# Two copies of the first group's kT, from VectorE to ScalarE

## The chip, the cores and the metric

The kernel runs on one core of one Trainium2 chip. A core has a matrix engine (TensorE, PE in the profile, with its weight loads as PEld), VectorE (DVE), ScalarE (ACT), GpSimd (POOL) and a queue engine (SyncE, SP), and 16 DMA engines. The metric is the device time of one launch in microseconds, as the median of several runs; a profile of one execution shows what each engine did.

## The reference

Sliding-window attention with four sink positions, then an MLP mixer over tokens and channels. Cut to what matters (B = 4 batches, H = 8 heads, S = 768 positions, D = 64):

```python
def _attn_ref(q, k, v, n_sink, window):        # n_sink = 4, window = 128
    scores = scale * np.matmul(q, k.transpose(0, 1, 3, 2))
    rel = pos[:, None] - pos[None, :]
    keep = (pos[None, :] < n_sink) | ((rel >= 0) & (rel < window))
    scores = np.where(keep, scores, -1000000000.0)
    a = np.exp(scores - max)
    a = a / (np.sum(a, axis=-1, keepdims=True) + 1e-09)
    return np.matmul(a, v)

def _moe_ref(x, w_tok1, w_tok2, w_ch1, w_ch2):  # x: heads side by side, 4 x 768 x 512
    xt = x.transpose(0, 2, 1)
    h = np.maximum(xt @ w_tok1, 0.0) @ w_tok2   # 768 -> 256 -> 768
    u = x + h.transpose(0, 2, 1)
    h2 = np.maximum(u @ w_ch1, 0.0) @ w_ch2     # 512 -> 1536 -> 512
    return u + h2
```

## The kernel before

The work is cut into eight groups of four heads (two groups make a batch), and a group into two pairs of heads (j = 0, 1). For each pair q and k are loaded as float32, cast to bfloat16, transposed by TensorE into a PSUM bank, and copied from there into qT and kT. Then come the scores, 128 keys at a time with the 256 queries that can see them, in three units a pair; an exp from PSUM into pT; and the product with v.

Which engine does the PSUM copies of the first batch stands in a table: one row for each pair (2 * group + j), and in it the engine of q and that of k. A tuple leaves the choice to a scheduler.

```python
FIRST_TURNS = [[('ACT', 'DVE'), 'ACT'], [('ACT', 'DVE'), 'DVE'], ['DVE', 'DVE'], ['DVE', 'ACT']]
SPLIT_TC = {(0, 1), (0, 0)}              # pairs whose copies are made in two halves
SIZES = [1, 1, 2, 2, 2, 2, 2, 3]         # units of scores in one task, by group
PE_MASKS = {(0, 1), (1, 0), (1, 1), (0, 0)}
...
# make_turn: six transposes into one bank, then the copies
m = add("PE", pe(*[P] * m_), f, [c[x] if parts > 1 else c, t_ident], prio=pr(g, "tr", j), need=("g", 1), slot=slot)
...
if (g, j) in SPLIT_TC:
    ...
    for y in range(2):
        G.T[w][j].append(add(FIRST_TURNS[2 * g + j][w], either(NT * P // 2), lambda t, y=y, eh=eh: eh(t, y), [m, *free],
                             prio=pr(g, "tc", j) + 0.01 * y, slot=slot, frees=y == 1))
    continue
```

In the first batch the mask is put in by TensorE: a product of the identity with a tile of large negative numbers (`mneg`) opens the accumulation, and the four score products go on top. The last task of a group also makes the scores of the sink positions from `ks`, two small copies out of kT, which wait for all of the group's kT:

```python
def f(t, todo=todo, slots=slots, first=first, early=early, fm=fm, sink_slot=sink_slot):
    if first and not early:
        fm(t)                                            # ident x mneg, two matmuls
    for (j, u), slot in zip(todo, slots):
        for kt, w in kts_of(u)[0]:
            for i in range(2):
                nc.tensor.matmul(half(slot, i)[:, at:at + w]..., qkT(kT, g, j)[...], qkT(qT, g, j)[...], ...)
    if sink_slot:
        for c in range(4):
            nc.tensor.matmul(flat(sink_slot)..., ks[s][...], qkT(qT, g, c % 2)[...], start=True, stop=True)
...
G.exp[j, u] = add("ACT", act(2 * w), e, [m, *oldpv], prio=pr(g, "ex", j), slot=slot, frees=True)
```

Scores go through two double banks (`ps_sa`, `ps_sb`), everything else through four single banks (`ps_ga` to `ps_gd`). A score unit can begin when the exp of the unit before it in its buffer is done. The product with v needs the exps, v, and for the later rows the sink values (`pka`, `vsink`):

```python
m = add("PE", cost, f, [*deps, *G.cv, *(G.burst if last else [])], prio=pr(g, "pv"), need=("x" if last else "g", 1), slot=slot)
```

v and the weights are loaded through GpSimd's queue, each such load waiting for the one eight places before it:

```python
LOADS = "v0 v1 tok1 ch1a ch1c tok2 ch1b ch2b k2 ch2a q2 v2 q3 k3 v3".split()
...
if eng == "POOL" and len(log) >= 8:
    deps.append(log[-8])
```

The order of instructions on each engine isn't written by hand. All work is added as tasks with dependencies, a priority (a long table of ranks) and an estimated length, and a greedy scheduler plays them through and writes down the order. The engines then run that fixed order, waiting where an input isn't there:

```python
t.prio = r                       # from the table of ranks
...
todo = plan.order()              # plays the tasks through by estimated lengths
for t in todo:
    t.fn(t)
```

So a change of an engine in one entry can move other instructions too, where the scheduler comes to another order.

Of the kernel before, what the change touches and what calls it, by code (L numbers as in the profile page):

```python
# [15 lines left out]
LOADS = "v0 v1 tok1 ch1a ch1c tok2 ch1b ch2b k2 ch2a q2 v2 q3 k3 v3".split()  # L16
CAST_LOADS = set()
HALVES = set()
FIRST_TURNS = [[('ACT', 'DVE'), 'ACT'], [('ACT', 'DVE'), 'DVE'], ['DVE', 'DVE'], ['DVE', 'ACT']]
K_QUEUE = ['ACT', 'ACT', 'ACT', 'ACT']  # L20
PE_MASKS = {(0, 1), (1, 0), (1, 1), (0, 0)}
DMA_TURNS = {5, 6, 7}
# [120 lines left out]
class Plan:  # L143
# [8 lines left out]
    def add(self, *a, **k):  # L152
        t = Task(*a, **k)
        self.tasks.append(t)
        return t
# [182 lines left out]
def either(n):  # L338
    return {"ACT": act(n) + ACT_MORE, "DVE": dve(n)}
# [3 lines left out]
def kernel(  # L343
# [282 lines left out]
    def pr(g, what, j=0):  # L626
        like = KIND.get(what, what)
        extra = BIAS.get(f"{what}{g}", 0) + (BIAS.get(f"{what}{g}.{j}", 0) if j else 0)
        if what == "ex" and g >= GB:
            extra += 20  # L630
        if g < GB:
            return FIRST[like] + 0.5 * g + extra
        return (g // GB) * 10 + CH[like] + 0.5 * (g % GB) + extra
# [91 lines left out]
    def make_turn(g, w):  # L725
# [11 lines left out]
        for j in range(2):  # L737
# [3 lines left out]
            for x in range(parts):  # L741
# [20 lines left out]
                if (g, j) in SPLIT_TC:  # L762
                    def eh(t, y, j=j, slot=slot):
                        ps = flat(slot).bitcast(BF16)[:, 0:NT * P].rearrange("d (t p) -> d p t", t=NT)
                        hp = P // 2
                        copy(t, T[s][:, ts(j, NT)].rearrange("d t p -> d (t p)").rearrange("d (p t) -> d p t", t=NT)[:, ds(hp * y, hp)], ps[:, ds(hp * y, hp)])
# [6 lines that stand above are left out]
                G.T[w][j].append(add(FIRST_TURNS[2 * g + j][w] if g < GB else ("ACT", "DVE"), either(m_ * P), e, [m, *free], prio=pr(g, "tc", j), slot=slot, frees=True))  # L773

# [745 lines left out]
```

## Time and profile before

| | us |
|---|---|
| time, median of 3 runs | 200.34 (200.27 to 200.4) |
| span of the profiled execution | 198.6 |
| VectorE busy | 137.8 |
| ScalarE busy | 109.0 |
| GpSimd busy | 84.8 |
| v of group 0, issue to landing | 13.5 |
| VectorE's two copies that the change concerns, 10.28 to 11.29 | 1.01 |

The profile names an instruction by its line in the kernel, its engine and what it writes and reads: L753 are the transposes, L443 copies and casts on VectorE or GpSimd, L441 those on ScalarE, L815 and L819 the masks, L832 the scores, L876 the exps, L863 the exp of the sink scores, L839 the sink scores, L936, L941 and L945 the products with v, L1011 and L1035 the token mixing, L1113 the channel mixing. Letters at the end of a name tell copies of a tile apart: kTa belongs to the even groups, kTb to the odd ones, pTa and pTb to the two pairs of an even group, pTc and pTd to those of an odd one. Start times are in us from the start of the span. A bracket at the end of a row says how long the engine stood idle before it and what ended that.

### The profile page before, as it was taken

What the parts mean: (1) busy time and instruction counts of PE and PEld (TensorE: products, weight loads), DVE (VectorE), ACT (ScalarE), POOL (GpSimd) and SP (SyncE); (2) the same over time, 40 slices, a digit from 0 to 9 for tenths busy, and PEclk for the clock granted to TensorE, in tenths of its full rate; (3) what the DMA queues carried; (4) which work ended last, traced back from release to release, by engine and by line L of the source; (5) the groups of instructions that cost most, each with busy time, mean ns of one, the idle gap of its engine ahead of it and who ended that gap; (6) DMA issues with size and microseconds to landing.
All of it is one profiled execution on the core that took longest, in us unless ns stands there. A gap on an engine that the chain in (4) does not pass through costs nothing.

```text
span 198.6 us, 4636 instructions
## 1 busy us (share of the span) xinstructions
PE 190.0 (96%) x1784; PEld 129.3 (65%) x1795; DVE 137.8 (69%) x323; ACT 109.0 (55%) x196; POOL 84.8 (43%) x148
## 2 busy tenths in 40 slices
PE   7788999999999999999999999999999999999992
PEld 2433786665667564665766787566778787567882
DVE  4598673567775668834568965468588969289973
ACT  2787558889999744187436201867846002855100
POOL 8995432005899953178571010892970000020000
PEclk9999999999999999999999999999999999999999
DMA  5999999999399979899999899250000149000043
GB/s 172 367 224 181 208 207 329 234 257 218 91 317 214 206 150 140 215 129 225 231 179 133 158 206 208 106 137 0 0 3 0 38 99 314 30 3 0 26 162 132
DMA packets 75015, 31.00 MB, mean 156 GB/s; under 512 B 63666, under 2 KB 71474, under 8 KB 74994
## 3 DMA queue, kind: packets, MB, share of 16 engines
q1 hardware_dynamic: 44082, 18.85, 42.0%
q0 software_dynamic: 29680, 10.22, 42.0%
q10 hardware_dynamic: 1232, 1.64, 2.3%
q8 instruction: 14, 0.23, 0.5%
q14 instruction: 7, 0.06, 0.1%
HBM read 26.77 MB, written 6.29 MB: 167 GB/s over the span
## 4 chain that ended last, share of the span: by engine, by line
PE 88%; DMA 7%; ACT 2%; issue 1%; DVE 1%; POOL 0%; DVEq 0%; POOLq 0%
PE ps_gb L1113 9%; PE ps_gd L1113 7%; PE ps_ga L1113 7%; DMA vaa<-in_v_dram 7%; PE ps_gd L1260 5%; PE ps_gb L1260 5%; PE ps_gc L1113 4%; PE ps_gc L1260 4%; PE ps_ga L1260 3%; PE ps_sa L1260 3%; PE ps_gd L1368 3%; PE ps_gc L1368 3%; PE ps_sa L832 2%; PE ps_sb L832 2%; PE ps_sb L1113 2%; PE ps_gd L1011 2%
## 5 line engine op out<-in xcount | busy, mean ns | idle before, releaser
L1113 PEld LDWEIGHTS <-w_ch 128*128 128x128 bf16 x352 | 33.1, 98 | 20.3 <-issue 0.6
L1260 PEld LDWEIGHTS <-v 128*128 128x128 bf16 x222 | 21.1, 98 | 4.1 <-issue 0.5
L1070 ACT ACTIVATE v<-ps_gb 128x384 bf16<-128x384 f32 x18 | 8.9, 493 | 12.8 <-PE ps_gb L1113 12.7
L1070 ACT ACTIVATE v<-ps_gc 128x384 bf16<-128x384 f32 x12 | 5.9, 491 | 16.0 <-PE ps_gc L1113 15.1
L1197 POOL TENSOR_SCALAR v<-q32b 128x384 bf16<-128x384 f32 x1 | 1.2, 1176 | 27.6 <-DVE q32b L1183 27.6
L887 POOL TENSOR_TENSOR pTa<-pTa,mask 128x512 bf16<-128x512 bf16 x2 | 2.3, 1155 | 21.9 <-ACT pTa L876 21.9
L1113 PE MATMUL ps_gd<-uTa,w_ch 128*128 128x384 bf16 x56 | 11.4, 326 | 0.0
L1070 ACT ACTIVATE v<-ps_ga 128x384 bf16<-128x384 f32 x18 | 8.8, 491 | 4.7 <-PE ps_ga L1113 4.6
L1113 PE MATMUL ps_gb<-uTa,w_ch 128*128 128x384 bf16 x56 | 11.4, 326 | 0.0
L1011 PEld LDWEIGHTS <-w_tok 128*128 128x128 bf16 x96 | 9.2, 98 | 1.8
L1070 ACT ACTIVATE v<-ps_gd 128x384 bf16<-128x384 f32 x15 | 7.4, 492 | 5.3 <-PE ps_gd L1113 5.0
L1368 PEld LDWEIGHTS <-v 128*128 128x128 bf16 x72 | 6.2, 98 | 6.2 <-issue 0.8
L1113 PE MATMUL ps_gb<-uTb,w_ch 128*128 128x384 bf16 x48 | 9.8, 326 | 0.0
L1072 DVE TENSOR_SCALAR v<-ps_gd 128x384 bf16<-128x384 f32 x7 | 3.9, 555 | 7.6 <-PE ps_gd L1113 7.6
L486 POOL DMA_DIRECT2D vaa<-in_v_dram x4 | 6.0, 1504 | 7.4 <-PE ps_gc L945 7.4
L1113 PE MATMUL ps_ga<-uTa,w_ch 128*128 128x384 bf16 x44 | 8.9, 326 | 0.0
L486 POOL DMA_DIRECT2D vab<-in_v_dram x4 | 5.8, 1453 | 6.2 <-PE ps_gb L1035 2.3
L1113 PE MATMUL ps_ga<-uTb,w_ch 128*128 128x384 bf16 x40 | 8.1, 326 | 0.0
L876 ACT ACTIVATE pTc<-ps_sb 128x768 bf16<-128x768 f32 (+1 forms) x6 | 5.5, 921 | 3.5 <-PE ps_sb L832 3.5
L876 ACT ACTIVATE pTb<-ps_sa 128x1024 bf16<-128x1024 f32 (+1 forms) x7 | 6.9, 989 | 0.5 <-PE ps_sa L832 0.5
L443 POOL CAST kbb<-k32b 128x768 bf16<-128x768 f32 x5 | 4.4, 884 | 5.5 <-DMA k32b<-in_k_dram 5.5
L443 POOL CAST qbb<-q32b 128x768 bf16<-128x768 f32 x5 | 4.4, 888 | 5.3 <-DMA q32b<-in_q_dram 5.3
(460 smaller groups left out, 587.9 us busy)
## 6 DMA issues: line engine op xcount, KB each, us to landing
q32a<-in_q_dram SPq DMA_DIRECT2D x4, 384.0 KB, 4.4
vaa<-in_v_dram POOLq DMA_DIRECT2D x4, 384.0 KB, 11.4
vab<-in_v_dram POOLq DMA_DIRECT2D x4, 384.0 KB, 11.4
w_ch<-in_moe_w_ch_dram POOLq DMA_DIRECT2D x3, 512.0 KB, 15.3
w_ch<-in_moe_w_ch_dram POOLq DMA_DIRECT2D x2, 768.0 KB, 19.7
q32b<-in_q_dram SPq DMA_DIRECT2D x8, 192.0 KB, 4.0
k32b<-in_k_dram SPq DMA_DIRECT2D x8, 192.0 KB, 3.7
out_dram<-oa SPq DMA_DIRECT2D x4, 256.0 KB, 3.5
```

The source lines that it names most:

```text
L443: on(t).tensor_copy(out=o, in_=i)
L486: t = add(eng, hold, lambda t: e.dma_start(out=o, in_=i), deps, prio=prio, dma=work, run=run)
L832: nc.tensor.matmul(half(slot, i)[:, at:at + w].rearrange("p (c q) -> p c q", q=P), qkT(kT, g, j)[ds(64 * i, 64), kt], qkT(qT, g, j)[ds(64 ...
L876: nc.scalar.activation(dst[:, :, 512 * u:512 * u + w], ps_s[slot.at[1]][:, :, 0:w], AF.Exp, scale=scale)
L887: on(t).tensor_tensor(out=dst[:, :, 0:2 * P], in0=dst[:, :, 0:2 * P], in1=mask0.rearrange("p i c q -> p i (c q)"), op=ALU.mult)
L1011: nc.tensor.matmul(flat(slot)[:, 0:GH * D], w_tok1[:, n, ts(tt, P)], x[:, n, ds(a * GH * D, GH * D)], start=(n == 0), stop=(n == NT - 1))
L1070: nc.scalar.activation(o, i, AF.Relu)
L1072: nc.vector.tensor_scalar(out=o, in0=i, scalar1=0.0, scalar2=None, op0=ALU.max)
L1113: nc.tensor.matmul(flat(slot)[:, 0:HS], w_ch1[:, c, ts(ft, P)], uT_[:, c, ds(half * HS, HS)], start=(c == 0), stop=(c == NC - 1))
L1197: nc.gpsimd.tensor_scalar(out=o, in0=i_, scalar1=0.0, scalar2=None, op0=ALU.max)
L1260: nc.tensor.matmul(flat(slot)[:, 0:cw], A[n][0][:, x, ts(i, P)], W[n][:, x, ds(c0, cw)], start=(first and x == 0), stop=(x == NH - 1), ski ...
L1368: nc.tensor.matmul(flat(slot)[:, 0:cw], v1[:, ft, ts(st, P)], w_ch2[:, ft, ds(c0, cw)], start=(ft == 0), stop=(ft == NF - 1 and (b > 0 or ...
```

## The change

One entry of the table: the copy of kT of group 0, second pair of heads, goes from VectorE to ScalarE. The pair is one of those that are copied in halves, so two instructions of 128x384 elements change engines. It is meant to take load from VectorE in the first microseconds, where it casts, copies and moves constants for both groups of the first batch. (The change carries the name "normalising of the last batch's attention in two tasks, ranks refitted"; that code and the ranks are the same in both kernels, and what differs is only this line.)

```diff
-FIRST_TURNS = [[('ACT', 'DVE'), 'ACT'], [('ACT', 'DVE'), 'DVE'], ['DVE', 'DVE'], ['DVE', 'ACT']]
+FIRST_TURNS = [[('ACT', 'DVE'), 'ACT'], [('ACT', 'DVE'), 'ACT'], ['DVE', 'DVE'], ['DVE', 'ACT']]
```

The scheduler makes a somewhat different order of it, in the first 20 us alone. Written as tasks, in order:

```
TensorE, before                          TensorE, after
scores group 0, pair 1, unit 0           scores group 0, pair 1, unit 0
scores group 0, pair 1, unit 1           transposes q, group 1, pair 0
transposes q, group 1, pair 0            scores group 0, pair 1, unit 1
transposes k, group 1, pair 0            transposes k, group 1, pair 0
scores group 0, pair 1, unit 2, sinks    scores group 0, pair 1, unit 2, sinks
transposes q, group 1, pair 1            transposes q, group 1, pair 1
product with v, group 0 (8 matmuls)      scores group 1, pair 0, 384 wide
transposes k, group 1, pair 1            product with v, group 0 (8 matmuls)
scores group 1, pair 0, 384 wide         transposes k, group 1, pair 1
scores group 1, pair 0, 512 wide         scores group 1, pair 0, 512 wide
```

On ScalarE the exp of the 384-wide unit of group 1 likewise goes ahead of the kT copy of group 1's second pair, and one of its two small copies into `ks` of group 0 goes to VectorE; one small copy for group 1 goes one place later. On VectorE, beside the copies taken away, the first normalising products stand one place apart among the constants' copies. GpSimd and SyncE keep their order.

## The prediction

> **What bounds the kernel now.** I read the page first, then the waits of TensorE, then the first 31 us in order of time, then GpSimd's queue of loads. The page says who is full:
>
> ```profile
> span 198.6 us, 4636 instructions
> ...
> PE 190.0 (96%) x1784; PEld 129.3 (65%) x1795; DVE 137.8 (69%) x323; ACT 109.0 (55%) x196; POOL 84.8 (43%) x148
> ...
> PE 88%; DMA 7%; ACT 2%; issue 1%; DVE 1%; POOL 0%; DVEq 0%; POOLq 0%
> ```
>
> TensorE has 8.6 us without a matmul, and the chain that ends last is 88% TensorE and 7% one transfer. Of the 8.6 us, 3.6 lie behind the last matmul (stores), 2.2 before the first 6 us are over. An entry that moves two copies from one half-empty engine to another can only matter in the few gaps left. TensorE's waits name them:
>
> ```profile
> PE ps_ga L1475 <- DVE warm L447: 1.2, 1, 1.2
> PE ps_ga L753 <- DVE kba L443: 1.1, 1, 1.1
> PE ps_gb L941 <- DMA vaa<-in_v_dram: 0.9, 1, 0.9
> PE ps_sa L819 <- ACT pTc L876: 0.4, 1, 0.4
> ```
>
> Columns: total, times, longest. The first two come before the changed copies. The third is the one to look at: TensorE stands 0.9 us because the first product of probabilities and v, which is next in its fixed order, needs v of group 0. That load is issued at 1.55 and takes 13.5 us (the DMA's 7% of the chain). The surroundings, in order of time (start, length, engine):
>
> ```profile
> 10.28 1.01 DVE L443 COPY kTa<-ps_gd 128x384 bf16<-128x384 bf16 x2
> 11.46 1.00 ACT L876 ACTIVATE pTb<-ps_sa 128x1024 bf16<-128x1024 f32 x1
> 13.74 0.51 PE L753 MATMUL ps_gd<-ident,qbb 128*128 128x128 bf16 x6
> 13.86 0.38 ACT L863 ACTIVATE pka<-ps_gc 128x256 bf16<-128x256 f32 x1 [0.49 <-PE ps_gc L839]
> 15.15 0.20 PE L941 MATMUL ps_gb<-vaa,pTa 128*128 128x65 bf16 x1 [0.90 <-DMA vaa<-in_v_dram]
> 15.40 0.50 PE L753 MATMUL ps_gc<-ident,kbb 128*128 128x128 bf16 x6
> 15.74 0.49 PE L819 MATMUL ps_sb<-mneg,ident 128*128 128x384 bf16 x2
> 15.94 0.81 ACT L441 ACTIVATE kTb<-ps_gc 128x768 bf16<-128x768 bf16 x1 [0.99 <-PE ps_gc L753]
> 16.43 0.39 PE L819 MATMUL ps_sa<-mneg,ident 128*128 128x512 bf16 x1
> 16.65 0.81 ACT L876 ACTIVATE pTc<-ps_sb 128x768 bf16<-128x768 f32 x1
> 17.70 1.02 ACT L876 ACTIVATE pTc<-ps_sa 128x1024 bf16<-128x1024 f32 x1
> 20.54 0.28 PE L936 MATMUL ps_gd<-vsink,pka 128*128 128x260 bf16 x1
> ```
>
> The first row is the two copies that the change moves. The gap ahead of 15.15 holds back TensorE, and ScalarE with it (0.99 us idle before 15.94). From 15.94 to 20.5 the two go hand in hand, exp after exp through two score buffers; from 20.54 on TensorE is full (7.60 of 7.60 us between 24.0 and 31.6).
>
> **What the Trainium skill says.** *Perfetto Trace Analysis*, Optimizing Scalar/DVE Operations: every instruction pays an access overhead, about 51 ns for ScalarE on PSUM and 125 ns for VectorE on PSUM, the recorded latency is longer because its tail overlaps the next instruction, and work may be moved to ScalarE where VectorE is full. The trace agrees for ScalarE: a 384-wide copy is recorded with 0.49 us, but the next instruction starts 0.37 us after it (8.04 to 8.41). On VectorE the two copies, from 10.28, let the next one start at 11.21, 0.465 each, less than 384 elements at its 0.96 GHz plus 125 ns (an estimate from that page and *VectorE: DVE Perf Modes*, Specifications: 0.525). The measured values are used. *VectorE: DVE Perf Modes*, the perf-mode tier table, allows copies from PSUM up to double rate; 0.465 us for 384 elements is 1.2 ns an element, so no doubling shows here, and VectorE is no faster than ScalarE at this copy. *Perfetto Trace Analysis*, Optimization Strategy: look for gaps on the fullest engine and make the dependency start sooner. The change can't make v land sooner; it can only put other work into the gap.
>
> **The change part by part.** Comparing the compiled orders, all that differs lies in the first 20 us; from there on each engine has the same instructions in the same order (bank names apart). GpSimd and SyncE don't change at all.
>
> 1. VectorE loses two 384-wide copies, 0.93 us (10.28 to 11.21), and gains one 64x8 copy for the sink keys, about 0.15. It casts group 1's q and k from about 10.3 rather than 11.21. It then stands until ScalarE's second half copy is done (step 2: 11.8), so its copies of group 1's first q and k start near 12.0 and 12.95, against 12.74 and 13.61: some 0.65 earlier.
>
> 2. ScalarE gains two copies of 0.37 and loses one of the small copies, (11.46 - 11.13)/2 = 0.165: net +0.58 us. Start to start, with 0.91 for a 1024-wide exp (8.41 to 9.32), 0.97 for the one before 10.29, 0.70 for a 768-wide one (an estimate from its 0.81 less 0.11 overlap), 0.28 for the sink exp (13.86 to 14.14): half copy 10.29, exp 10.66, half copy 11.36 (ending 11.85), exp of the next unit 11.73 (before 11.46), small copy, exp 12.80 (before 12.36), sink exp 13.9, exp 14.18 (before 14.14). Two idle stretches, 0.49 and 0.99 us in the rows above, take up the 0.58.
>
> 3. TensorE's order changes in two places. The second score unit of group 0's second pair of heads goes behind one batch of six transposes, which covers the later kT. And the 384-wide score unit of group 1 (the rows at 15.74) goes ahead of the product that waits for v. It needs kT of group 1 (step 1, about 13.9), and its buffer, free when the exp from 12.80 ends at 13.82. The six transposes at 13.74 precede it, so masks near 14.12, scores near 14.54 (16.16 - 15.74 = 0.42 later, as now), done by 14.9. That is before v lands at 15.10.
>
> 4. So after v lands TensorE still does the product (15.15) and six transposes (15.40), but at 15.74 it goes straight to the unit that now starts at 16.43: **0.69 us** of its work moves into the gap. ScalarE's 0.81 us exp of that unit (now 16.65) likewise moves into its gap, near 15.0. The kT copy stays at 15.94; the next exp starts near 16.8 instead of 17.70.
>
> 5. From there the alternation runs on. The exps now at 18.63, 19.74 and 20.66 come near 17.85, 18.8 and 19.9 (0.91 an exp, 0.17 for the small copy; 0.85 to 0.95 for a unit of TensorE), and TensorE is through with that unit near 19.8 instead of 20.54. VectorE's sink values, now ready at 18.37 + 1.29 = 19.66, are a floor just under that. Lead at this place: **0.74 us**.
>
> 6. From 20.54 on TensorE is its own limit, so the lead lives to the end unless a load, which doesn't move, becomes the last to arrive. The sum: 200.34 - 0.74 = 199.60; I take off 0.05 for the tight places of the third rival: **199.65 us**.
>
> **The rivals.** *First: ScalarE becomes the bound.* It is full between 8 and 12 (3.96 of 4.00 us), and gets 0.58 more there; were there no idle time after it, every exp would come 0.3 to 0.6 later, and with them the units behind: 200.6 to 200.9. Against it: the 0.49 and 0.99 us of idle time just behind, and step 2, where the delay is down to 0.04 by 14.18.
>
> *Second: VectorE's relief is worth nothing.* If kT of group 1 or the exp that frees the score buffer is late, the unit isn't done when v lands; then TensorE finishes it first, and the product comes later by as much as was saved. A unit started only at 15.0 would give 200.3. For it speaks that the margin in step 3 is only 0.2 us; against it, that each bit done before 15.10 is still won.
>
> *Third: the loads hide it.* GpSimd's queue keeps at most eight loads open, so its issues show when earlier ones land:
>
> ```profile
> 27.16 0.75 POOL L486 DMA_DIRECT2D k32b<-in_k_dram  x1 [1.12 <-DMA w_tok<-in_moe_w_tok_dram]
> 30.23 1.43 POOL L486 DMA_DIRECT2D vab<-in_v_dram  x1 [2.32 <-PE ps_gb L1035]
> ```
>
> The first waits for the second token weight: issued at 10.45, it takes 16.4 us, so it lands at 26.85. TensorE's first use is at 27.66, and would be at 26.9: nothing to spare. The issue at 30.23 waits, by the eight-load rule, for the third part of the channel weight; TensorE's first use, at 31.4, would move to 30.65. k of group 2 lands at 35.4 and is cast by 36.4; its transposes, at 37.3, would move to 36.5. All three just fit a lead of 0.74; a lead of 1 us would be cut. If one lands later than now, the time comes back to 199.8 to 200.2.
>
> **Range and chances.** The gap is 0.9 us, which caps the direct gain: 199.4, or 199.2 if ScalarE's idle time is used better than I think. Rival two or three in part gives 199.9 to 200.2. Eight in ten: 199.2 to 200.25. Two per cent are 4.0 us; nothing in the first 20 us that the change touches has that size, so within 2% has 0.98, and 0.01 on either side.
>
> **What would show it.** Right: group 1's 384-wide scores ahead of 15.1, TensorE's wait for v near 0.2 us (from 0.9), ScalarE's exp of them near 15.0, the sink product that starts at 20.54 now near 19.8, and a wait-free TensorE after it. Wrong: these scores behind 15.1 (step 3), exps behind 16 us no earlier than now (steps 2, 5), or a new wait of TensorE for a weight near 27, 31 or 36.5 (step 6). A longer v load would also break it, as everything hangs on its landing at 15.1.

## The result, and the profile after

The changed kernel takes 199.35 us (199.29 to 199.49) beside 200.37 us (200.27 to 200.5) for the kernel before, a ratio of 0.995 with a 95% interval of 0.9932 to 0.9967: about 1.0 us less. The page of the changed kernel:

```profile
span 197.8 us, 4635 instructions
...
PE 190.4 (96%) x1784; PEld 129.4 (65%) x1795; DVE 136.4 (69%) x322; ACT 109.3 (55%) x197; POOL 84.9 (43%) x148
```

Nothing of weight is different in the sums. VectorE is 1.4 us less busy and ScalarE 0.3 us more, TensorE has 7.4 us without a matmul instead of 8.6. The span is 0.8 us shorter, not 1.0: the profiled execution of the kernel before was its fastest (200.27), that of the changed one its slowest (199.49). TensorE's wait for v is still there, 0.6 us instead of 0.9, and its 0.4 us wait for an exp (`ps_sa L819 <- ACT pTc` in the prediction's list) is gone. The stretch in order of time (start, length, engine):

```profile
10.21 0.52 ACT L441 ACTIVATE kTa<-ps_gd 128x384 bf16<-128x384 bf16 x1
...
11.28 0.55 ACT L441 ACTIVATE kTa<-ps_gd 128x384 bf16<-128x384 bf16 x1
...
11.89 0.96 DVE L443 COPY qTb<-ps_gb 128x768 bf16<-128x768 bf16 x1
...
13.00 0.96 DVE L443 COPY kTb<-ps_ga 128x768 bf16<-128x768 bf16 x1
...
14.47 0.34 PE L832 MATMUL ps_sb<-qTb,kTb 64*128 64x256 bf16 x4
...
14.86 0.81 ACT L876 ACTIVATE pTc<-ps_sb 128x768 bf16<-128x768 f32 x1
15.37 0.19 PE L941 MATMUL ps_gb<-vaa,pTa 128*128 128x65 bf16 x1 [0.56 <-DMA vaa<-in_v_dram]
...
15.61 0.50 PE L753 MATMUL ps_ga<-ident,kbb 128*128 128x128 bf16 x6
...
16.15 0.81 ACT L441 ACTIVATE kTb<-ps_ga 128x768 bf16<-128x768 bf16 x1 [0.48 <-PE ps_ga L753]
...
16.91 1.02 ACT L876 ACTIVATE pTc<-ps_sa 128x1024 bf16<-128x1024 f32 x1
...
17.83 0.20 ACT L441 ACTIVATE ksb<-kTb 64x8 bf16<-64x8 bf16 x1
17.93 1.00 ACT L876 ACTIVATE pTc<-ps_sb 128x1024 bf16<-128x1024 f32 x1
...
19.83 0.28 PE L936 MATMUL ps_gd<-vsink,pka 128*128 128x260 bf16 x1
```

The first two rows are the two copies, now on ScalarE. VectorE's copies of group 1's q and k start at 11.89 and 13.00 (before 12.74 and 13.61); the 384-wide unit's scores are made at 14.47, ahead of v, and its exp is at 14.86 (before 16.65). Behind v TensorE goes from the product (15.37) to the transposes (15.61) and straight to the 512-wide unit. The sink product is at 19.83 instead of 20.54.

One thing is not as before although nothing changed it: v's product starts at 15.37 instead of 15.15, because the load, issued at 1.55 in both, took 13.78 us instead of 13.55. Everything behind hangs on that landing, so I measure leads from it. That this is fair is shown by f1, which differs from the kernel before by the place of one small copy: its v product comes 0.24 us later, its sink product 0.30 and its token mixing 0.29 later, and that execution took 200.58 us instead of 200.27. Two places serve: the sink product (L936), and the first token-mixing product of the second batch near 59 us.

| kernel | v product | sink product | token mixing, 2nd batch | from v to it | lead | median time |
|---|---|---|---|---|---|---|
| before | 15.15 | 20.54 | 59.45 | 44.30 | | 200.37 to 200.46 |
| changed | 15.37 | 19.83 | 58.63 | 43.26 | 1.04 | 199.35 |
| e1, order alone | 15.34 | 20.02 | 58.92 | 43.58 | 0.72 | 199.80 |
| e2, copies alone | 15.23 | 20.47 | 59.27 | 44.04 | 0.26 | 200.17 |
| f1, small copy later | 15.39 | 20.84 | 59.74 | 44.35 | -0.05 | 200.48 |
| f2, transposes ahead too | 15.41 | 19.53 | 58.49 | 43.08 | 1.22 | 199.44 |
| g1, order and small copy | 15.28 | 20.01 | 58.91 | 43.63 | 0.67 | 199.72 |
| g2, small copy ahead | 15.30 | 19.84 | 58.65 | 43.35 | 0.95 | 199.93 |
| h1, g1 with banks swapped | 15.29 | 20.03 | 58.93 | 43.64 | 0.66 | 200.50 |

Starts are in us from the profiled executions; the lead is 44.30 less the column before it. The changed kernel's 1.04 is what the medians show (1.02), and it comes in three parts: 0.71 from the order (e1, at the sink product), 0.22 from ScalarE's steps around one small copy, and 0.11 from two steps of ScalarE near 38 us. The next two sections take them in turn. Where the last column doesn't follow the lead (f2, g2, h1), time was lost after 59 us or in executions that weren't profiled; this is taken up below.

### The profile page after: what moved, and what is told of

It is laid out like the page before. It is cut to its first block, busy times and chain, and to the rows that moved or that the text cites. A ratio compares the mean times of both kernels' runs of the same rounds, so it can differ in the third digit from the quotient of the medians.

```text
span 197.8 us, 4635 instructions
## 1 busy us (share of the span) xinstructions
PE 190.4 (96%) x1784; PEld 129.4 (65%) x1795; DVE 136.4 (69%) x322; ACT 109.3 (55%) x197; POOL 84.9 (43%) x148
## 4 chain that ended last, share of the span: by engine, by line
PE 87%; DMA 7%; ACT 2%; issue 1%; DVE 1%; POOL 0%; DVEq 0%; POOLq 0%
PE ps_gc L1113 9%; DMA vaa<-in_v_dram 7%; PE ps_ga L1113 7%; PE ps_gd L1113 7%; PE ps_gd L1260 5%; PE ps_gc L1260 5%; PE ps_gb L1113 4%; PE ps_gb L1260 4%; PE ps_ga L1260 3%; PE ps_sa L1260 3%; PE ps_gd L1368 3%; PE ps_gb L1368 3%; PE ps_sa L832 2%; PE ps_sb L832 2%; PE ps_sb L1113 2%; PE ps_gd L1011 2%
## 5 line engine op out<-in xcount | busy, mean ns | idle before, releaser
L1070 ACT ACTIVATE v<-ps_gc 128x384 bf16<-128x384 f32 x19 | 9.4, 493 | 24.6 <-PE ps_gc L1113 23.7
L1113 PE MATMUL ps_gc<-uTa,w_ch 128*128 128x384 bf16 x56 | 11.4, 326 | 0.0
L1113 PE MATMUL ps_gc<-uTb,w_ch 128*128 128x384 bf16 x52 | 10.6, 326 | 0.0
L1072 DVE TENSOR_SCALAR v<-ps_gc 128x384 bf16<-128x384 f32 x9 | 5.0, 554 | 3.2 <-PE ps_gc L1113 3.0
L1070 ACT ACTIVATE v<-ps_gb 128x384 bf16<-128x384 f32 x11 | 5.4, 491 | 3.2 <-PE ps_gb L1113 3.2
## 6 DMA issues: line engine op xcount, KB each, us to landing
w_ch<-in_moe_w_ch_dram POOLq DMA_DIRECT2D x2, 768.0 KB, 19.8
```

The lines of the kernel that those rows point to most:

```text
L1070: nc.scalar.activation(o, i, AF.Relu)
L1072: nc.vector.tensor_scalar(out=o, in0=i, scalar1=0.0, scalar2=None, op0=ALU.max)
L1113: nc.tensor.matmul(flat(slot)[:, 0:HS], w_ch1[:, c, ts(ft, P)], uT_[:, c, ds(half * HS, HS)], start=(c == 0), stop=(c == NC - 1))
```

## The experiments

My theory was that the gain is the 0.69 us of TensorE's work moved into the gap ahead of v, and that the copies' change of engine only brings that order about. The rivals were that the copies' engines gain by themselves, and that the landing of v, or another load, sets the time whatever the order.

### The order alone, and the copies alone

e1 is the kernel before (VectorE keeps its copies) with the changed kernel's order for one unit; e2 is the changed kernel with that unit put back behind the transposes.

```diff
 todo = plan.order()
+unit, its_exp = Gs[1].burst[2], Gs[1].exp[0, 2]
+# e1, in the kernel before:
+move(unit, Gs[0].pv[1], 0);  move(its_exp, unit, 1)
+# e2, in the changed kernel:
+copy_k = Gs[1].T[1][1][0]
+move(unit, copy_k.deps[0], 1);  move(its_exp, copy_k, 1)
```

(`move(t, to, after)` puts a task ahead of or behind another; `pv[1]` is the product that waits for v.)

> The kernel before with the two copies of kT still on VectorE; only the 384-wide score unit of group 1 goes ahead of the product that waits for v, and its exp ahead of the kT copy of group 1's second pair. If the order is what pays: kT of group 1 is there near 14.6, the unit is done near 15.05, TensorE waits for v some 0.3 to 0.4 us instead of 0.9, and the time is 199.3 to 199.7. If VectorE's relief is needed for it, the unit comes after v has landed and the time stays at 200.2 to 200.4.

> The changed kernel with its two copies on ScalarE, but the 384-wide unit and its exp put back behind the product with v and the transposes. If the order is what pays: TensorE waits for v about 1.1 us (the wait after, 0.6, and the unit's 0.5 to 0.7), the time is 200.2 to 200.5. If the relief of VectorE pays by itself: 199.3 to 199.6.

Measured: e1 199.80 us (ratio 0.9977, 0.9965 to 0.9989; runs from 199.64 to 201.04), e2 200.17 us (0.9992, 0.9982 to 1.0003), with 200.44 for the kernel before beside them. The interval of e2 reaches past 1, so its time alone doesn't tell it from the kernel before, and the traces have to. By the leads, order 0.72 and copies 0.26, together 0.98 of 1.04. Order alone, in the stretch of e1 on TensorE and ScalarE:

```profile
14.60 0.34 PE L832 MATMUL ps_sb<-qTb,kTb 64*128 64x256 bf16 x4
...
15.34 0.19 PE L941 MATMUL ps_gb<-vaa,pTa 128*128 128x65 bf16 x1 [0.39 <-DMA vaa<-in_v_dram]
...
16.11 0.81 ACT L441 ACTIVATE kTb<-ps_gc 128x768 bf16<-128x768 bf16 x1 [0.32 <-PE ps_gc L753]
...
16.95 0.20 ACT L441 ACTIVATE ksb<-kTb 64x8 bf16<-64x8 bf16 x1
...
17.18 1.02 ACT L876 ACTIVATE pTc<-ps_sa 128x1024 bf16<-128x1024 f32 x1
...
18.10 1.02 ACT L876 ACTIVATE pTc<-ps_sb 128x1024 bf16<-128x1024 f32 x1
```

The unit is made at 14.60, ahead of v, with VectorE still doing all four copies: it is 0.13 later than in the changed kernel and early enough. So VectorE's relief is not needed for the order to pay; for this part the new entry mattered because the scheduler then chose this order. Nor does the landing set the time whatever the order: e1's v product is 0.19 later than before, and its sink product 0.52 earlier. This bears out the theory for the larger part. It does not for the 0.26 that the copies bring with the old order, where the wait for v stays at 0.8 us.

### Where the rest lies: a small copy

The two orders differ on ScalarE in one more thing. From the kTb copy to the second 1024-wide exp e1 takes 18.10 - 16.11 = 1.99 us, the changed kernel 17.93 - 16.15 = 1.78. That is 0.21 of the 0.22 by which their sink products differ, each counted from v (4.68 and 4.46). In this stretch stands the 64x8 copy `ksb`: behind the first exp in the changed kernel, ahead of it in e1. I first held its place for the cause: f1 moves it in the kernel before, g1 moves it in e1, g2 moves it back in the changed kernel.

```diff
+small = [t for t in Gs[1].ksc if t.on == "ACT"][0]
+move(small, Gs[1].exp[0, 0], 1)    # f1 (kernel before) and g1 (e1): behind the exp
+move(small, Gs[1].exp[0, 0], 0)    # g2 (changed kernel): ahead of it
```

> The kernel before, with nothing but one small copy into ks of group 1 on ScalarE put behind the exp that follows it, as in the changed kernel. If that place is what the run with the copies alone won: the exp now at 17.70 starts 0.2 to 0.3 earlier, the time is 0.15 to 0.3 below before. If that run won by VectorE's relief instead: the same as before within 0.05.

> The kernel before with the 384-wide score unit of group 1 ahead of the v product (as in e1_order_alone, 199.80 us) and, besides, ScalarE's small copy ksb behind the exp of the 512-wide unit in ps_sa (as the changed kernel has it). Theory that the small copy's place is what the order alone lacked: the exp of ps_sa starts 0.25 us earlier, the sink product follows the v product by about 4.45 us instead of 4.68, and the time is 199.45 to 199.6, that of the changed kernel. Rival, that the place is worth nothing here as in f1_small_copy_later, and that the copies of group 0's kT on ScalarE bring the rest themselves: 199.75 to 199.9.

> The changed kernel with ScalarE's small copy ksb put back ahead of the exp of the 512-wide unit in ps_sa. Theory that its place is worth the difference between the changed kernel and the order alone: the sink product follows the v product by about 4.7 us instead of 4.46, time 199.65 to 199.8. Rival, that the place is worth nothing: 199.4 to 199.5.

Measured: f1 200.48 us (1.0, 0.9992 to 1.0008), g1 199.72 (0.9965, 0.9954 to 0.9977), g2 199.93 (0.9977, 0.9966 to 0.9988; its two shortest runs, one of them the profiled one, are at 199.5, the other five at 199.9 to 200.3, and what those lost isn't in a profile). By its median alone g2 would speak for the place. By the leads f1 gains nothing, g1 is e1 again (0.67, 0.72), and g2 loses 0.09 of 1.04, with its sink product 4.54 us behind the v product where the theory asked for 4.7. So at most a small part is the place. The rows say where the rest is. ScalarE in g1:

```profile
16.81 1.02 ACT L876 ACTIVATE pTc<-ps_sa 128x1024 bf16<-128x1024 f32 x1
17.86 0.21 ACT L441 ACTIVATE ksb<-kTb 64x8 bf16<-64x8 bf16 x1
18.09 1.02 ACT L876 ACTIVATE pTc<-ps_sb 128x1024 bf16<-128x1024 f32 x1
```

and in g2:

```profile
16.92 0.21 ACT L441 ACTIVATE ksb<-kTb 64x8 bf16<-64x8 bf16 x1
17.03 1.00 ACT L876 ACTIVATE pTc<-ps_sa 128x1024 bf16<-128x1024 f32 x1
```

In g1 the small copy starts 1.05 us after the exp ahead of it, so not before that exp's 1.02 us are over, and the next exp 0.23 after the small copy. In the changed kernel the same two steps, in the same order, are 0.92 and 0.10. In g2, with the copy ahead, its step to the exp is 0.11, where e1 has 0.23. All kernels of the table above show 0.10 to 0.13 where the copies are on ScalarE, and 0.22 or 0.23 where they are on VectorE. The Trainium skill (*Perfetto Trace Analysis*, Optimizing Scalar/DVE Operations) gives about 93 ns of overhead for ScalarE on SBUF and a recorded latency of about twice that: 0.10 us from start to start and 0.20 us recorded agree, and 0.23 is what the page has no account of.

Two things about this copy differ between the two families. In the compiled programs of f1 and g1 it waits for VectorE's semaphore and ScalarE's own, in those of the changed kernel and e2 for its own alone, because there the kTb copy, reading a bank that VectorE used last, has already waited for VectorE. And the scheduler gives ScalarE rows 64 to 127 of ksb with the old table, GpSimd rows 0 to 63; with the new one it is the other way round. h1 takes the first away: two PSUM banks change names from the transposes of group 1's last k on, and the small copy then waits for one semaphore. Shortened, the edit is:

```diff
+# g1, and from the kbb transposes of group 1, second pair, on:
+if p == "g": sl.at = (p, [2, 1, 0, 3][b])      # ps_ga <-> ps_gc
```

> g1_order_and_small_copy (199.72 us) with nothing changed but two bank names: from the kbb transposes of group 1's second pair on, whatever was in ps_ga goes to ps_gc and the other way round. The kTb copy on ScalarE then reads the bank that VectorE read last, so this copy carries the wait for VectorE, and the small copy ksb behind it waits for one semaphore (ScalarE's own) instead of two, as in the changed kernel. Theory that the two waits cost the remainder: the small copy starts 0.92 us after the exp ahead of it instead of 1.05, the next exp 0.10 after the small copy instead of 0.23, the sink product follows the v product by about 4.45 us instead of 4.73, and the time is 199.4 to 199.5, that of the changed kernel. Rival, that the waits don't matter and the remainder comes from the copies' engines: 1.05 and 0.23 stay, 199.65 to 199.8.

Measured: 200.50 us (1.0, 0.9989 to 1.0011). ScalarE in h1:

```profile
16.83 1.02 ACT L876 ACTIVATE pTc<-ps_sa 128x1024 bf16<-128x1024 f32 x1
17.87 0.20 ACT L441 ACTIVATE ksb<-kTb 64x8 bf16<-64x8 bf16 x1
18.10 1.02 ACT L876 ACTIVATE pTc<-ps_sb 128x1024 bf16<-128x1024 f32 x1
```

1.04 and 0.23: the second wait is not what costs. The lead at 59 us is that of g1 (0.66), and the slower median comes later (below).

What remains is the half of the rows, and the other copies of this form bear it out. ScalarE makes about ten of them in each kernel, and the compiled program says which rows each one takes. In all 14 profiles, no copy of rows 64 to 127 starts before the instruction ahead of it has ended, and none of the instructions behind one starts before that copy has ended (0.01 us or more later). Behind a copy of rows 0 to 63 the next instruction starts 0.02 to 0.13 us before the copy's end, unless it is itself a copy of rows 64 to 127 or is held up by something else. The changed kernel has both: rows 0 to 63 at 17.83, with 0.10 to the next exp, and rows 64 to 127 at 38.71 (ScalarE, then TensorE):

```profile
37.15 0.81 ACT L441 ACTIVATE kTa<-ps_ga 128x768 bf16<-128x768 bf16 x1
37.84 0.84 ACT L441 ACTIVATE qba<-q32a 128x768 bf16<-128x768 f32 x1
38.71 0.21 ACT L441 ACTIVATE ksa<-kTa 64x8 bf16<-64x8 bf16 x1
38.94 0.49 ACT L1070 ACTIVATE v<-ps_gd 128x384 bf16<-128x384 f32 x1
...
39.19 0.50 PE L753 MATMUL ps_gb<-ident,qba 128*128 128x128 bf16 x6
39.52 0.81 PE L1113 MATMUL ps_gd<-uTa,w_ch 128*128 128x384 bf16 x4
```

The copy at 38.71 starts 0.87 us after a cast of 0.84 us, and the next instruction 0.23 after the copy. So 0.22 of the lead lies in the two steps around group 1's small copy, and neither its second wait nor, but for a small part, its place accounts for it. That it is the half of the rows fits every copy in the record, but no kernel here changed the half alone, and why it should matter is open.

The last 0.11 lies elsewhere. From the sink product to the token mixing at 59 us it takes 38.90 or 38.91 us in the five kernels of the table with the old entry, and 38.80 or 38.81 in the changed kernel, e2 and g2. The same stretch in the kernel before shows where it goes:

```profile
37.87 0.81 ACT L441 ACTIVATE kTa<-ps_ga 128x768 bf16<-128x768 bf16 x1
38.69 0.84 ACT L441 ACTIVATE qba<-q32a 128x768 bf16<-128x768 f32 x1
...
39.79 0.49 ACT L1070 ACTIVATE v<-ps_gd 128x384 bf16<-128x384 f32 x1
...
39.90 0.50 PE L753 MATMUL ps_gc<-ident,qba 128*128 128x128 bf16 x6
40.33 0.81 PE L1113 MATMUL ps_gd<-uTa,w_ch 128*128 128x384 bf16 x4
```

The cast of q starts 0.82 us after the kT copy, when that has ended; in the changed kernel it starts 0.69 after it. What follows on ScalarE is late by as much, up to the relu that empties ps_gd (39.79 + 0.49 = 40.28). TensorE needs that bank, so it starts 0.43 us behind its transposes instead of 0.33. The step is 0.82 or 0.83 in all six kernels with the old entry and 0.69 in all with the new one. Neither instruction is a copy of half the rows, and both wait for the same things in both programs; the reason is open.

### Is the rest of the gap worth filling?

f2 also takes the six transposes of group 1's last k ahead of the product that waits for v; f3 takes the masks and scores of the 512-wide unit with them. f4 is the changed kernel again, as their companion.

```diff
+move(Gs[1].T[1][1][0].deps[0], Gs[0].pv[1], 0)     # f2 and f3
+move(Gs[1].burst[0], Gs[0].pv[1], 0)               # f3 alone
```

> The changed kernel, with the six transposes of group 1's last k ahead of the product that waits for v too. If any work done before v lands is won one for one: TensorE's wait shrinks by 0.34, the time is 0.25 to 0.4 below the changed kernel, near 199.0. If the exps set the pace before 20 us: the same as the changed kernel within 0.1.

> As the last one, and the next 512-wide score unit ahead of the product as well; the wait for v should be gone. If the gap is all that is to be won: 0.5 to 0.6 below the changed kernel, near 198.8. If the sink values (ready at 19.97) or the loads behind (second token weight at 26.85, third part of the channel weight at 30.0, k of group 2 cast at 36.4) take over: no better than the last one, and a wait of TensorE for one of them shows.

> The changed kernel as it is, beside the others on one chip: 199.3 to 199.5 by both theories. It shows how the landing of v and the time scatter from execution to execution.

Measured: f2 199.44 us (0.9951, 0.9937 to 0.9966), f3 199.81 (0.9975, 0.9965 to 0.9984), f4 199.44 (0.9947, 0.9933 to 0.9961). f2 hardly waits for v any more (its transposes end at 15.26, v lands at 15.37), and its sink product is 0.30 earlier than f4's (19.53 against 19.83), but its time is the same; at 31 us only 0.14 of the 0.30 is left. TensorE and GpSimd in f2:

```profile
26.48 0.33 PE L1032 MATMUL ps_gc<-ident,x_ba 128*128 128x128 bf16 x3
26.80 0.48 PE L1035 MATMUL ps_gc<-w_tok,h1a 128*128 128x384 bf16 x2
```

```profile
10.39 0.72 POOL L486 DMA_DIRECT2D w_tok<-in_moe_w_tok_dram  x1
...
27.04 0.75 POOL L486 DMA_DIRECT2D k32b<-in_k_dram  x1 [1.12 <-DMA w_tok<-in_moe_w_tok_dram]
```

The first product with the second token weight (L1035) starts 0.32 us after the transposes ahead of it; the next pair, at 27.12 and 27.29, has 0.17. The weight, issued at 10.39, took 16.4 us, so it landed at 26.8, when that product starts. This is the third rival of the prediction, and it begins just beyond the changed kernel, whose product starts at 26.94 with 0.16 behind its transposes.

f3 turns the gain into a new wait, the longest of those that the changed kernel doesn't have:

```profile
PE ps_gd L936 <- DVE vsink L595: 0.8, 1, 0.8
```

With the product with v later, VectorE's normalising and then its sink values (18.68 in the changed kernel, 19.40 here) come later, and now they, not the exps, hold the sink product.

g3 tries f2 with the second token weight issued ahead of the first parts of the channel weight (shortened):

```diff
+move(L["tok2"], L["ch1a"], 0)        # with f2's line
```

> f2_turn_ahead (changed kernel with the last kbb transposes ahead of the v product) with the second token weight's load issued ahead of the first two parts of the channel weight, near 8.9 us instead of 10.4. Theory that this load's landing at 26.8 took back 0.15 of the 0.30 us that f2_turn_ahead had won: landing near 25.3, first L1035 product 0.16 us behind the transposes ahead of it instead of 0.32, first channel mixing near 30.4, time 199.25 to 199.35. Rival, that the channel weight's first parts, now 0.7 us later, take it instead, or that something else stood there: 199.4 to 199.7.

Measured: 199.81 us (0.9963, 0.9952 to 0.9974). The runs lie between 199.05 and 200.31: four at 199.05 to 199.24, a little below what was expected, and eleven above 199.5. The profiled execution (200.20) is one of the latter, and shows another cause. GpSimd and VectorE in g3:

```profile
9.82 2.45 POOL L486 DMA_DIRECT2D w_ch<-in_moe_w_ch_dram  x3
12.26 0.84 POOL L443 CAST qbb<-q32b 128x768 bf16<-128x768 f32 x1
13.03 0.84 POOL L443 CAST kbb<-k32b 128x768 bf16<-128x768 f32 x1
...
11.92 1.98 DVE L443 COPY ksa<-kTa 64x8 bf16<-64x8 bf16 x1
```

and in the changed kernel:

```profile
11.07 0.80 POOL L486 DMA_DIRECT2D w_ch<-in_moe_w_ch_dram  x1
...
11.52 0.34 DVE L443 COPY ksa<-kTa 64x8 bf16<-64x8 bf16 x1
```

The 64x8 copy `ksa` is the one that the new entry moved to VectorE. It takes 1.98 us in g3 and ends at 13.90, with GpSimd's two casts (13.03 + 0.84 = 13.87). VectorE's copies of q and k behind it come 1.8 to 2 us later, TensorE waits 0.7 us for kTb, and the lead is gone. The Trainium skill (*SBUF — State Buffer*, Who interferes with whom) says that VectorE in its two-port modes and GpSimd lock one pair of SBUF ports against each other for a whole instruction, and that the one which issues first gets it. The rows agree. In both kernels GpSimd is in the middle of issuing a load when the copy starts. In the changed kernel that ends at 11.87, the copy at 11.86, and GpSimd's first cast comes only at 12.15; the same form of copy takes 0.15 us at 38.85, with no work of GpSimd beside it. In g3 the casts follow the load without a gap, and the copy gets through only behind them.

Which way it goes is a matter of hundredths of a microsecond: in f2 and g2 the first cast starts at 11.86 and 11.88 and the copy still takes 0.35, and in e2, with the cast at 11.88 too, it takes 1.98:

```profile
11.10 0.80 POOL L486 DMA_DIRECT2D w_ch<-in_moe_w_ch_dram  x1
...
11.54 1.98 DVE L443 COPY ksa<-kTa 64x8 bf16<-64x8 bf16 x1
```

It costs e2 nothing that shows, since the scores that need VectorE's copies come only behind v there (16.24). The kernel before has no such copy on VectorE in this stretch, so the new entry has brought in a risk: with the scores ahead of v, as in g3, the standstill takes the lead away. It may be what the slower runs of f2, g2 and g3 lost, but those executions weren't profiled, and no run varied the two engines' work there on purpose. g3 isn't a version that beats the changed kernel by its median, and that the weight's landing took half of f2's lead is shown only by f2's own rows.

### Can v come earlier?

e3 and e4 put the load of v first in GpSimd's queue, in the changed kernel and in the one before.

```diff
+for t in L["v0"]:
+    t.prio = -1000
```

> The changed kernel with the load of v of group 0 as GpSimd's first instruction, issued near 0.8 instead of 1.55. If the landing of v is still what TensorE stands for after the change: v lands 0.3 to 0.7 earlier, the wait of 0.6 shrinks by as much, the time is 198.7 to 199.1. If after the change the score buffers and exps set the pace before 20 us: 199.2 to 199.5, with v landing earlier and nothing gained.

> The kernel before with the load of v of group 0 as GpSimd's first instruction. If everything behind the landing of v moves with it one for one: v lands 0.3 to 0.7 earlier and the time is 199.6 to 200.0, the same gain as in the changed kernel or more, as the wait here is 0.9. If not: 200.2 to 200.4.

Measured: 212.11 us (1.0583, 1.0568 to 1.0597) and 213.56 (1.0653, 1.0639 to 1.0667). Neither tests the question. GpSimd in e3:

```profile
1.31 1.66 POOL L486 DMA_DIRECT2D vaa<-in_v_dram  x1 [0.81 <-POOLq L1503]
...
15.19 0.20 POOL L717 MEMSET vaa<- 128x24 bf16 x1 [11.99 <-DMA vaa<-in_v_dram]
...
16.54 0.86 POOL L486 DMA_DIRECT2D w_tok<-in_moe_w_tok_dram  x1
```

The load writes a tile whose column of ones GpSimd fills by a memset. With the load first, that memset waits for the landing (11.99 us idle), and the identity matrix and the masks stand behind it; TensorE waits 12.4 us for its first transposes. But the row is of use for v: issued at 1.31, it landed near 15.1, with none of GpSimd's weight loads issued before 16.54. In the kernel before, issued at 1.55, with the weights from 4.0 us on, it landed at 15.10 too. The weights behind it in the queue aren't what makes this load last 13.6 us.

### Losses further back

e1's and h1's runs scatter over more than 1 us. In e1's profiled execution (200.43) the lead is there at 59 us and gone at 73, and the chain says why:

```profile
53.95 6.88 DMA q32a<-in_q_dram
...
60.85 0.59 DVE qba L443
61.43 0.34 DVE h1b L1072
```

The load of q of group 4 (second half) takes 6.88 us. VectorE's fixed order has its cast (60.85) ahead of the relu (61.43) that TensorE needs, so TensorE waits 0.6 us at L839 (61.82). In h1 the same load takes 6.42 us and TensorE waits 0.4; in the changed kernel's profile it takes 5.9 and there is no wait. Each of these is one execution; whether the other slow runs of e1 and h1 lost their time in the same place isn't shown. It lies far behind the change, and is the reason for going by the leads at 59 us.

## Why the prediction was right, point by point

Predicted were 199.65 us, measured 199.35; the interval of the ratio on 200.37 is 199.0 to 199.7, so the prediction lies at its upper end. The mechanism was right and the size a little small.

- *Steps 1 and 2* hold within 0.15 us. VectorE's copies: 12.0 and 12.95 said, 11.89 and 13.00 measured. The small copy that VectorE gains was put at 0.15 us and took 0.34, beside GpSimd; that it could take 1.98 there was not foreseen. ScalarE's row of half copy, exp, half copy, exp: 10.29, 10.66, 11.36, 11.73 said, 10.21, 10.58, 11.28, 11.65 measured; the delay at the exp behind the sink exp was to be 0.04, and is -0.03 (14.11 against 14.14). The first rival, ScalarE as the bound, is out.
- *Step 3* holds: scores at 14.54 said, 14.47 measured, their exp at 14.86, v at 15.37. The second rival is out by more margin than I gave it: e1 shows that the unit would have been in time (14.60, v at 15.34) even without VectorE's relief.
- *Step 4*, 0.69 us moved into the gap, is what e1 measures by itself: 0.71 at the sink product.
- *Step 5* hits every start (17.85, 18.8, 19.9 said; 17.93, 18.94, 19.94 measured; the sink product 19.8 and 19.83), but by two errors that cancel: v landed 0.22 later than before, and the stretch behind it was shorter than said. **The mis-sized term is this step's lead of 0.74**: counted from v it is 5.39 - 4.46 = 0.93 at the sink product. The 0.19 us between the two in single pieces: from the kTb copy to the next exp I had 0.86, it took 0.76; that exp and the small copy behind it 1.05, they took 1.02; from there to the sink product 1.95, and it took 1.90; the rest is rounding. So half of it is the step from the kTb copy to the exp, which g1 shows as 0.76 too (16.05 to 16.81). My 19.8 - 15.15 = 4.65 agrees with what the order alone gives (e1: 4.68), but by luck: I had the step behind the kTb copy too long and, at 0.17, the small copy's cost too short for the old table. There exp and small copy take 1.05 and 0.23 (g1). What I had not seen is that the new table also changes which small copy ScalarE makes, and that with it the two steps are 0.92 and 0.10. That the sink values would be a floor just under the sink product was not met in the changed kernel, but f3 ran into it.
- *Step 6*: the lead lives to the end, as said; the 0.05 that I took off for tight loads was not needed. The third rival, a lead of 1 us being cut by the second token weight, is real but sets in a little later than I said, at f2's 1.22 us. The rest of the distance, from 0.93 at the sink product to 1.04 at 59 us, is ScalarE's shorter step near 38 us, of which the prediction had nothing.
- One sign was misread beforehand: TensorE's wait for v was to shrink to 0.2 us and is 0.6 and, in f4, 0.4. A later landing makes that wait longer and the gain no smaller; and in f4 the unit ahead of v is done 0.15 later than in the changed kernel's first profile, v lands at the same time, and the token mixing starts at 58.63 in both. So the size of the wait is no measure of what was gained.

## What to carry to other kernels

When a fixed order makes the fullest engine wait for a load, look for work whose inputs are ready and put it ahead of the waiting instruction; here 0.7 us of such work was worth 0.7 us, whoever did the copies. Measure the gain from the event that everything hangs on, here v's landing, since its own scatter of 0.2 us is a good part of a gain of 1 us. After each such step look for the next arrival: 0.3 us further on a weight was already late. And look at what else the change has moved: here a small copy came to stand beside GpSimd's work, where it can take 2 us.

## What the runs showed of the hardware that was not expected

- Two 64x8 copies of the same form on ScalarE cost 0.10 to 0.13 us or 0.22 to 0.23 us to the next instruction, with 0.92 or 1.05 us from the exp ahead of them. The longer steps go with rows 64 to 127, the shorter with rows 0 to 63, in every copy of the 14 profiles; the number of semaphores is not the reason, and the half was never changed alone.
- Two ScalarE instructions over all 128 rows, a kT copy and a cast behind it, stand 0.82 us apart with the old table entry and 0.69 with the new one; the reason is open.
- A 64x8 copy on VectorE takes 0.15 us with GpSimd idle, 0.34 or 0.35 beside the issue of a load on GpSimd, and 1.98 where two casts follow that issue on GpSimd and it loses to them (e2, g3). With the first cast at 11.86 to 11.88, it lost in one profile (e2) and won in three (f2, f3, g2).
- The 384 KB load of v takes 13.5 to 14.0 us from issue to landing, and in e3, with no other load of GpSimd's queue beside it until 16.5 us, no less. The same load for group 1, issued there at 18.97, took 6.4 us, when the first batch's q and k had landed; that these make the difference was not tried.
